# The block-diagonal stage of a long convolution, moved from full-array matmuls to sets of 32x32 array tiles

## The chip, the cores and the metric

The kernel runs on one core of one Trainium2 chip. The metric is device time in microseconds (us), measured for the whole execution; each kernel was run several times and the median is quoted. Every ratio below compares a kernel with the kernel before in the same rounds on the same chip. One core has no sibling cores to compare clocks with, so a run counts as undisturbed when it lies near the fastest of its kernel.

## The reference, cut to what matters

Two independent computations share the core. Part A is a gated long convolution over 2048 positions and 1024 channels, done by a transform of length 4096. Part B is a diagonal state space model (SSM) whose scan and dense products need none of A's results. The outputs are concatenated.

```python
# A: k_shift = short causal filter of k;  kv = k_shift * v
y_f = rfft(kv padded to 2S) * rfft(ssm_k padded to 2S)
y   = irfft(y_f)[:S] + kv * ssm_D
a   = q * y
# B: Bu = x @ B_bar^T ; h_t = Lam_bar * h_{t-1} + Bu_t ; y = 2 Re(h @ C^T) + x * Dskip
return concatenate([a, b], axis=-1)
```

## The kernel before

The transform is split into two steps. Step one multiplies by a dense 128-row matrix (stage A1) and writes a spectrum to DRAM (`Ys_kv`, `Ys_h`). Step two mixes only 32 numbers at a time (16 complex values), so 128 partitions hold four independent blocks, and its matrix is block-diagonal after a permutation. This middle stage, A2, loads both spectra, applies step two to each (`a2_s2`), multiplies them as complex numbers, applies the inverse of step two (`a2_sa`), and writes `Vs`. Stage A3 finishes the inverse. SSM work is interleaved with all of this by "ticks": the program puts operations on a list for each tick, and a scheduler then fixes each engine's order when it compiles.

The complex product needs real and imaginary halves exchanged. `ha` holds the filter's spectrum with the real parts in partitions 0 to 63 and the imaginary parts in 64 to 127; `hb` is the same with halves swapped, and the swap is two DMAs.

```python
    def dma(out_, in_):   return nc.sync.dma_start(out_, in_)     # issued by SP
    def dmas_(out_, in_): return nc.gpsimd.dma_start(out_, in_)   # issued by GpSimd (POOL)
    ...
    def a2_load(gq):                      # two of 32 groups at a time
        ...
        for nm, Ys in (("l2k", Ys_kv), ("l2h", Ys_h)):
            t_ = a2.tile([P, GC, D], BF16, name=nm, bufs=3)
            dma(t_[:], Ys.rearrange("c n (s g) d -> (c n s) g d", g=NG)[:, g0:g0 + GC, :])
        ...
        dma(wts[:], W3v[:, g0:g0 + GC, :, :])
    def a2_s2(g, src, dh):
        ...
        pt = ps_a.tile([P, 512], F32, name="psa")
        nc.tensor.matmul(pt[:], wts[:, gi, 0, :], s_[:, gi, dh * 512:(dh + 1) * 512], start=True, stop=True)
        nc.scalar.copy(d_[:, dh * 512:(dh + 1) * 512], pt[:])
        if src == 0 and dh == NH - 1:
            hb = a2.tile([P, D], BF16, name="hb", bufs=4)
            dmas_(hb[0:64, :], ha[64:128, :])
            dmas_(hb[64:128, :], ha[0:64, :])
    ...
    def a2_sa(g, dh):
        ...
        nc.tensor.matmul(pt[:], wts[:, gi, 1, :], ha[...], start=True, stop=False)
        nc.tensor.matmul(pt[:], wts[:, gi, 2, :], hb[...], start=False, stop=True)
        nc.scalar.copy(vsb[:, gi, dh * 512:(dh + 1) * 512], pt[:])
```

## Time and profile before

Median 431.73 us over three runs (428.91 to 433.8). I call "the stage" the time from the start of the first block-diagonal matmul to the start of the last one, read from the trace.

| before | value |
|---|---|
| stage | 190.4 to 361.8 us, 171.4 us, 16 pairs of groups |
| span of the profiled run | 431.1 us |
| busy in 183 to 366: TensorE / VectorE / ScalarE | 177.9 / 140.5 / 133.5 of 183 us |
| time after the stage | 69.3 us |

The view by windows gives, for each stretch, busy time and instruction count by engine, then the granted clock, the DMA share (1.0 would be all 16 DMA engines busy throughout) and the rate.

```profile
core 0: us, PE busy (x) PEld busy (x) DVE busy (x) ACT busy (x) POOL busy (x), PEclk, DMA share, GB/s
191.00:193.00 2.00, 2.00 (x23) 1.29 (x20) 2.00 (x5) 1.72 (x4) 0.57 (x2) 1.00 1.07 409
183.00:366.00 183.00, 177.91 (x1562) 110.92 (x1561) 140.51 (x241) 133.49 (x244) 47.49 (x89) 0.99 0.70 222
```

TensorE (PE) is busy for 178 of 183 us: it bounds the stage.

The timeline of TensorE (start, duration, source line, tiles, count) shows a full-array matmul here: the next instruction starts 0.216 us after it (241.70 to 241.92, 242.37 to 242.58).

```profile
241.70 0.38 PE L508 MATMUL psa<-l2h,wts 128*128 128x512 bf16 x1
241.92 0.61 PE L274 MATMUL pu<-xT,BT 128*128 128x128 bf16 x8
242.37 0.38 PE L532 MATMUL psa<-ha,wts 128*128 128x512 bf16 x1
242.58 0.38 PE L533 MATMUL psa<-hb,wts 128*128 128x512 bf16 x1
```

The page's list of DMA issues gives size and median time from issue to landing:

```profile
l2k<-Ys_kv SPq DMA_DIRECT2D x16, 512.0 KB, 6.0
l2h<-Ys_h SPq DMA_DIRECT2D x16, 512.0 KB, 4.2
hb<-ha POOLq DMA_DIRECT2D x64, 128.0 KB, 3.7
Vs<-vsb POOLq DMA_DIRECT2D x16, 512.0 KB, 5.9
```

### The profile page before, as it was taken

Reading aid. Unit: us, or ns where it says so; the run is one execution under the profiler, and the core shown is the slowest. Engines: PE = TensorE matmul, PEld = TensorE weight load, DVE = VectorE, ACT = ScalarE, POOL = GpSimd, SP = SyncE. Lnnn points to the kernel's source line nnn. Section 1 sums busy time; section 2 is a strip of 40 time slices with the busy share of each in tenths; the row PEclk is TensorE's granted clock in tenths of the full one; section 3 lists DMA queues with packets and bytes.
Section 4 is the critical chain, followed back from the end, with each engine's and each line's share of the span. In section 5 each row is a group of like instructions: output and inputs, shape, how many; then the busy total and the mean of one; then the engine's idle time right before and its main releaser. Section 6 shows DMA issues by size and latency. Waiting matters only on the chain.

```text
span 431.1 us, 9757 instructions
## 1 busy us (share of the span) xinstructions
PE 380.7 (88%) x3713; PEld 259.7 (60%) x3713; DVE 350.7 (81%) x642; ACT 303.6 (70%) x531; POOL 130.2 (30%) x224
## 2 busy tenths in 40 slices
PE   2589799797987997999899999999899999997784
PEld 2578687575765875775556566566465666763331
DVE  2989999999999999936897979797959637976830
ACT  1977999787886887646678877878568783344451
POOL 4000344464654455311222232322122211012121
PEclk9979999999999899999999999999899999999989
DMA  7879987778776544397778687879666523959981
GB/s 247 285 255 309 336 289 254 265 240 249 276 235 205 167 163 159 120 334 238 229 241 263 217 247 245 265 234 295 195 217 181 165 69 135 298 176 396 403 316 73
DMA packets 41353, 102.23 MB, mean 237 GB/s; under 512 B 6621, under 2 KB 8925, under 8 KB 41306
## 3 DMA queue, kind: packets, MB, share of 16 engines
q1 hardware_dynamic: 27322, 58.60, 42.7%
q0 software_dynamic: 13984, 43.01, 28.8%
q8 instruction: 29, 0.48, 0.5%
q14 instruction: 18, 0.15, 0.1%
HBM read 59.64 MB, written 33.55 MB: 216 GB/s over the span
## 4 chain that ended last, share of the span: by engine, by line
PE 42%; DVE 28%; issue 12%; DMA 10%; ACT 5%; POOL 2%; SPq 0%; POOLq 0%; DVEq 0%; ACTq 0%
PE pu L274 13%; PE py L345 13%; DVE m L409 5%; PE psa L508 5%; DVE acc L410 4%; DMA hb<-ha 3%; PE psa L533 3%; PE psa L532 3%; DVE ta L305 2%; DVE tb L308 2%; DVE acc L414 2%; DMA out_dram<-ot 2%; POOL out_dram L88 2%; DMA bn<-in_B_C_re_dram 1%; PE pt L601 1%
## 5 line engine op out<-in xcount | busy, mean ns | idle before, releaser
L274 PE MATMUL pu<-xT,BT 128*128 128x128 bf16 x2048 | 156.1, 222 | 0.5 <-ACT xT L263 0.3
L274 PEld LDWEIGHTS <-BT 128*128 128x128 bf16 x2048 | 136.2, 100 | 33.5 <-issue 2.4
L345 PE MATMUL py<-CT,h 128*128 128x512 bf16 x512 | 140.2, 382 | 2.3 <-ACT yo L355 2.3
L345 PEld LDWEIGHTS <-h 128*128 128x128 bf16 x512 | 46.7, 98 | 45.5 <-issue 4.9
L88 POOL DMA_DIRECT2D hb<-ha x64 | 33.4, 526 | 88.9 <-ACT ha L509 85.0
L534 ACT CAST vsb<-psa 128x512 bf16<-128x512 f32 x64 | 37.0, 602 | 25.7 <-PE psa L533 24.8
L88 POOL DMA_DIRECT2D Ys_h<-ysbh x64 | 45.6, 716 | 30.8 <-ACT ysbh L475 29.4
L277 ACT CAST u<-pu 128x512 bf16<-128x512 f32 x64 | 39.4, 615 | 13.2 <-PE pu L274 13.1
L428 ACT CAST ysb<-psa 128x512 bf16<-128x512 f32 x64 | 38.5, 644 | 13.7 <-PE psa L427 13.3
L519 DVE TENSOR_TENSOR ha<-x,ha 128x1024 bf16<-128x1024 bf16 x32 | 21.9, 684 | 27.8 <-DMA hb<-ha 18.7
L475 ACT CAST ysbh<-psa 128x512 bf16<-128x512 f32 x64 | 38.7, 641 | 5.5 <-issue 2.3
L509 ACT CAST ha<-psa 128x512 bf16<-128x512 f32 x64 | 36.8, 598 | 7.3 <-PE psa L508 6.3
L509 ACT CAST x<-psa 128x512 bf16<-128x512 f32 x64 | 36.9, 593 | 7.3 <-PE psa L508 5.2
L308 DVE TENSOR_TENSOR_SCAN tb<-rtab,tb 128x1024 bf16<-128x1024 f32 x16 | 36.6, 2285 | 0.0
L305 DVE TENSOR_TENSOR_SCAN ta<-rtab,ta 128x1024 bf16<-128x1024 f32 x16 | 36.5, 2280 | 0.0
L427 PE MATMUL psa<-acc,F1t 128*128 128x512 bf16 x64 | 24.6, 392 | 12.0 <-DVE acc L414 11.9
L564 ACT CAST ot<-psa 128x512 bf16<-128x512 f32 x32 | 17.9, 589 | 24.4 <-DMA out_dram<-ot 14.8
L409 DVE TENSOR_TENSOR m<-krow,wbc 128x1024 bf16<-128x1024 bf16 x48 | 32.4, 675 | 0.0
L410 DVE TENSOR_TENSOR acc<-acc,m 128x1024 bf16<-128x1024 bf16 x48 | 32.3, 673 | 0.0
L532 PE MATMUL psa<-ha,wts 128*128 128x512 bf16 x64 | 24.5, 384 | 4.2 <-DVE ha L519 4.0
L88 POOL DMA_DIRECT2D Ys_kv<-ysb x32 | 17.8, 557 | 33.9 <-ACT ysb L428 33.9
L350 PE MATMUL py<-Dd,xT 128*128 128x128 bf16 x128 | 28.0, 219 | 0.0
(139 smaller groups left out, 628.5 us busy)
## 6 DMA issues: line engine op xcount, KB each, us to landing
Ys_kv<-ysb POOLq DMA_DIRECT2D x32, 256.0 KB, 2.9
Ys_h<-ysbh POOLq DMA_DIRECT2D x64, 128.0 KB, 3.3
l2k<-Ys_kv SPq DMA_DIRECT2D x16, 512.0 KB, 6.0
l2h<-Ys_h SPq DMA_DIRECT2D x16, 512.0 KB, 4.2
hb<-ha POOLq DMA_DIRECT2D x64, 128.0 KB, 3.7
Vs<-vsb POOLq DMA_DIRECT2D x16, 512.0 KB, 5.9
vv<-Vs SPq DMA_DIRECT2D x32, 256.0 KB, 6.6
xn<-in_B_x_dram SPq DMA_DIRECT2D x16, 256.0 KB, 4.3
```

The costliest lines, as they stand in the source:

```text
L88: return nc.gpsimd.dma_start(out_, in_)
L274: nc.tensor.matmul(pu[:, c, jl, :], BT[:, j, c, dd, :], xT[:, dd, :], start=(dd == 0), stop=(dd == ND - 1))
L277: nc.scalar.copy(u[:, :, j - 1:j + 1, :], pu[:])
L305: ops.append(lambda: nc.vector.tensor_tensor_scan(fl(st["ta"]), fl(rtab), fl(st["ta"]), 0.0, ALU.mult, ALU.add))
L308: nc.vector.tensor_tensor_scan(fl(st["tb"]), fl(rtab), fl(st["tb"]), 0.0, ALU.mult, ALU.add)
L345: nc.tensor.matmul(py[:], h[:, c, j, :], CT[:, j, c, dh * 512:(dh + 1) * 512], start=(j == 0 and c == 0), stop=(j == NJ - 1 and c == 1))
L409: ops.append(lambda jj=jj: nc.vector.tensor_mul(st["m"][:], krows[n2 - jj][:], wbc[:, jj, :]))
L410: ops.append(lambda: nc.vector.tensor_add(st["acc"][:], st["acc"][:], st["m"][:]))
L428: nc.scalar.copy(ysb[:, dh * 512:(dh + 1) * 512], pt[:])
L475: nc.scalar.copy(ysbh[:, :, n2l, :], pt[:].rearrange("p (c d) -> p c d", c=2))
L509: nc.scalar.copy(d_[:, dh * 512:(dh + 1) * 512], pt[:])
L532: nc.tensor.matmul(pt[:], wts[:, gi, 1, :], ha[:, dh * 512:(dh + 1) * 512], start=True, stop=False)
```

## The change

The stage's weight matrix is three quarters zeros. The change drops the zeros: each 128x128 matmul becomes four matmuls of 32 partitions into 32 output rows, on four different 32x32 tiles of the array. Four groups together make a set of 16 tiles that covers the array and writes four PSUM banks. A unit is now four groups by 512 channels; there are again 16 units. To make it fit: block s must lie in partitions 32s to 32s+31, so the loads' source gets a separate dimension for s; the swap of halves becomes eight DMAs of 16 partitions; the transposes' PSUM pool gives one bank to the stage; and the DRAM spectra get a channel-half dimension.

```diff
-    ps_t = ctx.enter_context(tc.tile_pool(name="ps_t", bufs=2, space=PSUM))
+    ps_t = ctx.enter_context(tc.tile_pool(name="ps_t", bufs=1, space=PSUM))
-    ps_a = ctx.enter_context(tc.tile_pool(name="ps_a", bufs=3, space=PSUM))
+    ps_a = ctx.enter_context(tc.tile_pool(name="ps_a", bufs=4, space=PSUM))
 ...
-    Vs = tc.dram_tile([2, N2, P, D], BF16, name="Vs")          # Ys_kv, Ys_h alike
+    Vs = tc.dram_tile([NH, 2, N2, P, 512], BF16, name="Vs")
 ...
-            dma(t_[:], Ys.rearrange("c n (s g) d -> (c n s) g d", g=NG)[:, g0:g0 + GC, :])
+    ysv = {nm: t_.rearrange("h c n (s g) d -> h s (c n) g d", g=NG) ...}
+            dma(st[nm][:], ysv[nm][dh, :, :, qd * Q4:(qd + 1) * Q4, :])
 ...
+    def tiles16(outs, wt, rhs, u, inv, start, stop):
+        g0 = (u // NH) * Q4
+        for i in range(Q4):
+            for s_ in range(4):
+                a_, b_ = 32 * s_, 32 * ((s_ + i) % 4)
+                if inv:
+                    a_, b_ = b_, a_
+                nc.tensor.matmul(outs[i][b_:b_ + 32, :], a2state["w"][a_:a_ + 32, g0 + i, wt, :],
+                                 rhs[a_:a_ + 32, i, :], start=start, stop=stop)
 ...
-            dmas_(hb[0:64, :], ha[64:128, :])
-            dmas_(hb[64:128, :], ha[0:64, :])
+            for s_ in range(8):
+                o = s_ ^ 1
+                dmas_(hb[16 * s_:16 * s_ + 16, :, :], d_[16 * o:16 * o + 16, :, :])
 ...  (four evictions per set, products over 128x2048, one Vs store per unit, ticks per unit instead of per group)
```

More of the change, by code (lines that the diff above doesn't have):

```diff
@@ L34, in a_constants @@
     cph, sph = np.cos(phi), np.sin(phi)
-    W2 = np.zeros((2, 4, N2, NG, 2, 4, N2))
-    Wa = np.zeros((2, 4, N2, NG, 2, 4, N2))
-    Wb = np.zeros((2, 4, N2, NG, 2, 4, N2))
+    W3 = np.zeros((4, 2, N2, NG, 3, 2, N2))
     for si in range(4):
-        c_ = cph[si]; s_ = sph[si]
-        c_n2k2 = np.transpose(c_, (1, 0, 2)); s_n2k2 = np.transpose(s_, (1, 0, 2))
-        W2[0, si, :, :, 0, si, :] = c_n2k2
-        W2[1, si, :, :, 0, si, :] = s_n2k2
-        W2[0, si, :, :, 1, si, :] = -s_n2k2
-        W2[1, si, :, :, 1, si, :] = c_n2k2
-        c_k2n2 = np.transpose(c_, (2, 0, 1)); s_k2n2 = np.transpose(s_, (2, 0, 1))
-        Wa[0, si, :, :, 0, si, :] = c_k2n2
-        Wa[0, si, :, :, 1, si, :] = s_k2n2
-        Wa[1, si, :, :, 0, si, :] = -c_k2n2
-        Wa[1, si, :, :, 1, si, :] = -s_k2n2
-        Wb[0, si, :, :, 0, si, :] = -s_k2n2
-        Wb[0, si, :, :, 1, si, :] = c_k2n2
-        Wb[1, si, :, :, 0, si, :] = -s_k2n2
-        Wb[1, si, :, :, 1, si, :] = c_k2n2
+        for gi in range(NG):
+            c_, s_ = cph[si, gi], sph[si, gi]
+            r = (si + gi) % 4
+            W3[si, 0, :, gi, 0, 0, :] = c_
+            W3[si, 1, :, gi, 0, 0, :] = s_
+            W3[si, 0, :, gi, 0, 1, :] = -s_
+            W3[si, 1, :, gi, 0, 1, :] = c_
+            W3[r, 0, :, gi, 1, 0, :] = c_.T
+            W3[r, 0, :, gi, 1, 1, :] = s_.T
+            W3[r, 1, :, gi, 1, 0, :] = -c_.T
+            W3[r, 1, :, gi, 1, 1, :] = -s_.T
+            W3[r, 0, :, gi, 2, 0, :] = -s_.T
+            W3[r, 0, :, gi, 2, 1, :] = c_.T
+            W3[r, 1, :, gi, 2, 0, :] = -s_.T
+            W3[r, 1, :, gi, 2, 1, :] = c_.T
     f = lambda a: np.ascontiguousarray(a.reshape(128, -1), dtype=np.float32).astype(ml_dtypes.bfloat16)
-    W2 = np.transpose(W2, (0, 2, 1, 3, 4, 5, 6))
-    Wa = np.transpose(Wa, (0, 1, 2, 3, 4, 6, 5))
-    Wb = np.transpose(Wb, (0, 1, 2, 3, 4, 6, 5))
-    W3 = np.stack([W2.reshape(128, NG, 128), Wa.reshape(128, NG, 128), Wb.reshape(128, NG, 128)], axis=2)
     return f(F1), f(G), f(W3)
@@ L116, in full_kernel @@
     dma(Gt[:].rearrange("p c k -> p (c k)"), Gd.ap())
-    W3v = W3d.ap().rearrange("p (g t m) -> p g t m", g=NG, t=3)
-    Ys_kv = tc.dram_tile([2, N2, P, D], BF16, name="Ys_kv")
-    Ys_h = tc.dram_tile([2, N2, P, D], BF16, name="Ys_h")
-    Vs = tc.dram_tile([2, N2, P, D], BF16, name="Vs")
+    Ys_kv = tc.dram_tile([NH, 2, N2, P, 512], BF16, name="Ys_kv")
+    Ys_h = tc.dram_tile([NH, 2, N2, P, 512], BF16, name="Ys_h")
+    Vs = tc.dram_tile([NH, 2, N2, P, 512], BF16, name="Vs")
     praw = const.tile([4 * NJ, P], BF16, name="praw")
@@ L429, in a1_kv_mm @@
         if dh == NH - 1:
-            dmas_(Ys_kv[c, n2, :, :], ysb[:])
+            dmas_(Ys_kv[:, c, n2, :, :].rearrange("h k d -> k h d"), ysb[:].rearrange("k (h d) -> k h d", h=NH))
             A1.pop(("ysb", n2))
@@ L477, in a1h_mm @@
             for c in range(2):
-                dmas_(Ys_h[c, 2 * n2g:2 * n2g + 2, :, qd * DQ:(qd + 1) * DQ].rearrange("n k d -> k n d"), ysbh[:, c, :, :])
+                dmas_(Ys_h[qd // 2, c, 2 * n2g:2 * n2g + 2, :, (qd % 2) * DQ:(qd % 2 + 1) * DQ].rearrange("n k d -> k n d"), ysbh[:, c, :, :])
             A1.pop(("ysbh", qd, n2g))
@@ L481, in a1h_mm, with a2_load @@
                 A1.pop(("hT", qd, n2 // 4))
-    GC = 2
     a2state = {}
-    gstate = {}
-    def a2_load(gq):
+    Q4 = 4
+    ysv = {nm: t_.rearrange("h c n (s g) d -> h s (c n) g d", g=NG) for nm, t_ in (("l2k", Ys_kv), ("l2h", Ys_h))}
+    vsv = Vs.rearrange("h c n (s g) d -> h s (c n) g d", g=NG)
+    def a2_load(u):
         a2 = pools["a2"]
-        g0 = gq * GC
-        l2 = []
-        for nm, Ys in (("l2k", Ys_kv), ("l2h", Ys_h)):
-            t_ = a2.tile([P, GC, D], BF16, name=nm, bufs=3)
-            dma(t_[:], Ys.rearrange("c n (s g) d -> (c n s) g d", g=NG)[:, g0:g0 + GC, :])
-            l2.append(t_)
-        wts = a2.tile([P, GC, 3, P], BF16, name="wts", bufs=3)
-        dma(wts[:], W3v[:, g0:g0 + GC, :, :])
-        a2state[gq] = [l2[0], l2[1], wts, None]
@@ L499, in a2_s2 @@
-    def a2_s2(g, src, dh):
-        a2 = pools["a2"]
-        gq, gi = divmod(g, GC)
-        l2k, l2h, wts, _ = a2state[gq]
-        if src == 0 and dh == 0:
-            gstate[g] = [a2.tile([P, D], BF16, name="x16", bufs=4), a2.tile([P, D], BF16, name="ha", bufs=4), None]
-        x16, ha, _ = gstate[g]
-        s_, d_ = ((l2h, ha), (l2k, x16))[src]
-        pt = ps_a.tile([P, 512], F32, name="psa")
-        nc.tensor.matmul(pt[:], wts[:, gi, 0, :], s_[:, gi, dh * 512:(dh + 1) * 512], start=True, stop=True)
-        nc.scalar.copy(d_[:, dh * 512:(dh + 1) * 512], pt[:])
-        if src == 0 and dh == NH - 1:
-            hb = a2.tile([P, D], BF16, name="hb", bufs=4)
-            dmas_(hb[0:64, :], ha[64:128, :])
-            dmas_(hb[64:128, :], ha[0:64, :])
-            gstate[g][2] = hb
@@ L516, in a2_prod @@
-    def a2_prod(g, which):
-        x16, ha, hb = gstate[g]
-        if which == 0:
-            nc.vector.tensor_mul(ha[:], x16[:], ha[:])
-        else:
-            nc.vector.tensor_mul(hb[:], x16[:], hb[:])
-    def a2_sa(g, dh):
-        a2 = pools["a2"]
-        gq, gi = divmod(g, GC)
-        l2k, l2h, wts, vsb = a2state[gq]
-        if vsb is None:
-            vsb = a2.tile([P, GC, D], BF16, name="vsb", bufs=2)
-            a2state[gq][3] = vsb
-        x16, ha, hb = gstate[g]
-        pt = ps_a.tile([P, 512], F32, name="psa")
-        nc.tensor.matmul(pt[:], wts[:, gi, 1, :], ha[:, dh * 512:(dh + 1) * 512], start=True, stop=False)
-        nc.tensor.matmul(pt[:], wts[:, gi, 2, :], hb[:, dh * 512:(dh + 1) * 512], start=False, stop=True)
-        nc.scalar.copy(vsb[:, gi, dh * 512:(dh + 1) * 512], pt[:])
-        if dh == NH - 1:
-            gstate.pop(g)
-            if gi == GC - 1:
-                g0 = gq * GC
-                dmas_(Vs.rearrange("c n (s g) d -> (c n s) g d", g=NG)[:, g0:g0 + GC, :], vsb[:])
-                a2state.pop(gq)
+        qd, dh = divmod(u, NH)
@@ new lines, in a2_load @@
+        st = a2state[u] = {}
+        for nm in ("l2h", "l2k"):
+            st[nm] = a2.tile([P, Q4, 512], BF16, name=nm, bufs=3)
+            dma(st[nm][:], ysv[nm][dh, :, :, qd * Q4:(qd + 1) * Q4, :])
[6 more added lines that the diff above has]
+                    a_, b_ = b_, a_
+                nc.tensor.matmul(outs[i][b_:b_ + 32, :], a2state["w"][a_:a_ + 32, g0 + i, wt, :], rhs[a_:a_ + 32, i, :],
+                                 start=start, stop=stop)
@@ new lines, in a2_s2 @@
+    def a2_s2(u, src):
+        a2 = pools["a2"]
+        st = a2state[u]
+        nm = ("l2h", "l2k")[src]
+        d_ = st[("ha", "x16")[src]] = a2.tile([P, Q4, 512], BF16, name=("ha", "x16")[src], bufs=2)
+        pts = [ps_a.tile([P, 512], F32, name="psa") for _ in range(Q4)]
+        tiles16(pts, 0, st.pop(nm), u, False, True, True)
+        for i in range(Q4):
+            nc.scalar.copy(d_[:, i, :], pts[i][:])
+        if src == 0:
+            hb = st["hb"] = a2.tile([P, Q4, 512], BF16, name="hb", bufs=2)
+            for s_ in range(8):
+                o = s_ ^ 1
+                dmas_(hb[16 * s_:16 * s_ + 16, :, :], d_[16 * o:16 * o + 16, :, :])
@@ new lines, in a2_prod, with a2_sa @@
+    def a2_prod(u, which):
+        st = a2state[u]
+        t_ = st[("ha", "hb")[which]]
+        nc.vector.tensor_mul(t_[:], st["x16"][:], t_[:])
+    def a2_sa(u):
+        a2 = pools["a2"]
+        qd, dh = divmod(u, NH)
+        st = a2state.pop(u)
+        pts = [ps_a.tile([P, 512], F32, name="psa") for _ in range(Q4)]
+        tiles16(pts, 1, st["ha"], u, True, True, False)
+        tiles16(pts, 2, st["hb"], u, True, False, True)
+        vsb = a2.tile([P, Q4, 512], BF16, name="vsb", bufs=2)
+        for i in range(Q4):
+            nc.scalar.copy(vsb[:, i, :], pts[i][:])
+        dmas_(vsv[dh, :, :, qd * Q4:(qd + 1) * Q4, :], vsb[:])
@@ L548, in a3_load @@
             t_ = a3.tile([P, D], BF16, name=f"vv{c}", bufs=4)
-            dma(t_[:], Vs[c, n2, :, :])
+            dma(t_[:].rearrange("k (h d) -> k h d", h=NH), Vs[:, c, n2, :, :].rearrange("h k d -> k h d"))
             vv.append(t_)
@@ L722, in switch_a2 @@
             pools["a2"] = cms["a2"].__enter__()
+            a2state["w"] = pools["a2"].tile([P, NG, 3, 32], BF16, name="W3t", bufs=1)
+            dma(a2state["w"][:].rearrange("p g t m -> p (g t m)"), W3d.ap())
             a2_load(0)
@@ L726, in full_kernel @@
         a2_last = 0
-        for g in range(NG):
-            b = A2_T0 + g * A2_STEP
-            if g % GC == 0 and g // GC + 2 < NG // GC:
-                at(b, "misc", lambda g=g: a2_load(g // GC + 2))
-            for bi_, (src, dh) in enumerate([(0, 0), (0, 1), (1, 0), (1, 1)]):
-                at(b + bi_ // 2, "pe_a", lambda g=g, src=src, dh=dh: a2_s2(g, src, dh))
-            at(b + 3, "dve_a", lambda g=g: a2_prod(g, 0))
-            at(b + 3, "dve_a", lambda g=g: a2_prod(g, 1))
-            for dh in range(NH):
-                at(b + 5, "pe_a", lambda g=g, dh=dh: a2_sa(g, dh))
+        NU = NG // Q4 * NH
+        for u in range(NU):
+            b = A2_T0 + u * A2_STEP * 2
+            if u + 2 < NU:
+                at(b, "misc", lambda u=u: a2_load(u + 2))
+            at(b, "pe_a", lambda u=u: a2_s2(u, 0))
+            at(b + 1, "pe_a", lambda u=u: a2_s2(u, 1))
+            at(b + 3, "dve_a", lambda u=u: a2_prod(u, 0))
+            at(b + 3, "dve_a", lambda u=u: a2_prod(u, 1))
+            at(b + 5, "pe_a", lambda u=u: a2_sa(u))
             a2_last = max(a2_last, b + 5)
```

## The prediction

> **What bounds the kernel now.** The block-diagonal stage runs from about 183 us (first spectrum load) to 362 us (its last matmul), some 177 us for 16 pairs of groups, 11.1 us per pair. The busy time by window (183 to 366 us) gives TensorE 178 of 183 us, VectorE 141, ScalarE 133, granted clock 0.99. So TensorE bounds this stage; from 50 to 150 us VectorE does (49 of 50). In the timeline the stage's 128x512 matmuls start 0.216 us apart: 256 of them are 55 us of the 177; the rest is the SSM's.
>
> **What the change removes.** 256 full-array matmuls become 1024 of 32x32x512 in 64 sets of 16. [...] Weight loads fall from 3.1 MB to 0.8 MB.
>
> **What it does not remove.** ScalarE still makes 192 evictions of 128x512 (0.59 us each, the psum tile's view), VectorE the same products. Per unit of four groups, 12 evictions (7.1 us) now come in two ticks of four. Each set takes all four banks, so the next waits for evictions, 2.4 us per four. In the compiled order many sets are broken into fours of one bank between SSM matmuls; such fours should gain little. TensorE gives back most of its gain as waits on ScalarE. The halves' swap becomes 8 small DMAs per unit; at about 0.5 us of GpSimd issue each (0.524 now) the last is issued some 4 us after the first, and the products wait.
>
> **What I expect to decide: DMA engines.** The spectrum loads' source is no longer one stride over 128 rows: in the compiled program it is 4 x 32 x 2048 elements against 128 x 1 x 2048. [...] Saturated stretches show 391 to 404 GB/s at a share of 1.02 to 1.05, 24.5 GB/s an engine; a 4 KB packet takes 159 ns undisturbed. Per unit two 512 KB loads put 64 packets on each of four engines, 10.2 us; the swap, Vs stores and SSM traffic add about 3.2 us there. 13.4 us x 16 = 214 us, against 177: about +37 us, nearly all on the critical path since program order ties the SSM work to these ticks. Imperfect overlap, waits on the swap, one transpose bank instead of two at the start (+3 us) and 1 KB instead of 2 KB runs in Ys_kv stores and the last stage's loads (+2 us) add some 8 us.
>
> **Predicted: 476 us, 436 to 512 (8 in 10).** Faster by over 2%: 0.10; within 2%: 0.09; slower by over 2%: 0.81.
>
> **What would show it.** l2h and l2k landings rise from 4.2 and 6.0 us to 10 us or more; mean DMA share in the stage falls from 0.70 while tiled matmuls wait on these loads; the stage lasts 210 us or more; evictions keep 0.59 us; first transposes wait for evictions.
>
> **What would make it wrong.** If the loads still spread over 16 engines (landing under 7 us), bursts of evictions and the swap set the stage: 415 to 455 us. If moreover the sets of 16 overlap fully and waits are hidden, the next bounds are VectorE and ScalarE: about 410 to 420. If the Vs stores fall on four engines too and collide, over 500.

The sum: 431.7 before, 37 for the loads and 8 for the rest are the 476 us predicted. That the loads would get four engines no trace of the kernel before shows; the trace of the changed kernel does (a share of 0.27, below). The +3 and +2 us and the 8 us are estimates.

## More of the kernel before

While spectrum loads run (191 to 193), all 16 DMA engines are in use: a share of 1.07, at 409 GB/s.

The chain of work that ended last, by engine (shares of the span), is mostly TensorE and VectorE:

```profile
PE 42%; DVE 28%; issue 12%; DMA 10%; ACT 5%; POOL 2%; SPq 0%; POOLq 0%; DVEq 0%; ACTq 0%
```

## The result, and the profile after

The changed kernel takes 534.27 us (531.54 to 534.8). The ratio to the kernel before is 1.2346, with a 95% interval of 1.2251 to 1.2442. Such ratios are the mean time of one kernel's fast runs over that of the other's fast runs of the same rounds, so they are not quite the ratio of the quoted medians. Executions over 1.5% slower than the fastest of the same kernel are left out of the means. The direction was predicted; the size was not: 534 lies outside 436 to 512.

The windows show where the time is. The second line is the stage (199.3 to 459.1, 259.8 us instead of 171.4).

```profile
192.00:194.00 2.00, 2.00 (x28) 1.53 (x26) 0.00 (x0) 0.00 (x0) 0.00 (x0) 1.00 0.27 82
199.00:459.00 260.00, 217.65 (x2454) 115.78 (x2453) 163.93 (x247) 132.52 (x246) 77.86 (x153) 0.89 0.48 139
470.00:480.00 10.00, 4.69 (x25) 2.01 (x23) 0.00 (x0) 0.58 (x1) 0.56 (x1) 1.00 0.30 79
```

TensorE is now busy for 84% of the stage, not 97%. While little but spectrum loads runs (192 to 194), the DMA share is 0.27 at 82 GB/s: 0.27 x 16 = 4.3, about four of sixteen engines. Near the end of the inverse (470 to 480), while the last `Vs` stores land, the share is 0.30 at 79 GB/s: about four again (0.30 x 16 = 4.8).

The list of DMA issues. The page gives no landing time for the two loads (more on that below); the store's has doubled, and the swap's, at half the size, has doubled too:

```profile
l2h<-Ys_h SPq DMA_DIRECT2D x16, 512.0 KB
l2k<-Ys_kv SPq DMA_DIRECT2D x16, 512.0 KB
hb<-ha POOLq DMA_DIRECT2D x128, 64.0 KB, 7.2
Vs<-vsb POOLq DMA_DIRECT2D x16, 512.0 KB, 11.2
```

For the loads the trace has something better than the page: each increment of the semaphore that tells of a landing. A load of the kernel before makes 16 increments as it lands. Each of these loads makes one as its issue ends and four much later, which agrees with the four engines of the share. The last of the four comes 26.9 us (`l2h`) and 22.7 us (`l2k`) after the start of the issue, at the median, against 4.2 and 6.1 before.

The chain that ended last now runs through transfers, by engine and then by line:

```profile
DMA 34%; PE 23%; issue 13%; DVE 12%; ACT 12%; POOL 4%; SPq 1%; POOLq 0%; ACTq 0%; DVEq 0%
DMA l2h<-Ys_h 10%; DMA Vs<-vsb 10%; PE py L338 6%; PE pu L267 6%; PE psa L496 6%; DMA hb<-ha 5%; DMA Ys_h<-ysbh 4%; ACT ysbh L468 2%; DMA bn<-in_B_B_re_dram 2%; ACT vsb L528 2%; POOL out_dram L82 1%; ACT CT L618 1%; DVE ha L517 1%; DVE hb L517 1%; DVE ta L298 1%
```

The timeline of TensorE shows what became of the "sets of 16":

```profile
240.18 0.40 PE L496 MATMUL psa<-l2k,W3t 32*32 32x512 bf16 x4 [0.72 <-ACT vsb L528]
240.51 0.23 PE L267 MATMUL pu<-xT,BT 128*128 128x128 bf16 x1
240.67 0.40 PE L496 MATMUL psa<-l2k,W3t 32*32 32x512 bf16 x4
241.00 0.23 PE L267 MATMUL pu<-xT,BT 128*128 128x128 bf16 x1
...
242.19 0.39 PE L338 MATMUL py<-CT,h 128*128 128x512 bf16 x1
246.65 0.61 PE L496 MATMUL psa<-l2h,W3t 32*32 32x512 bf16 x4 [4.08 <-DMA l2h<-Ys_h]
```

The compiled order puts an SSM matmul between fours of one set, so each four pays its own time, 0.33 us here (240.18 to 240.51, 240.67 to 241.00). Then TensorE waits 4.08 us for a spectrum load.

Finally the waits of 189 to 471 us (engine, line and what ended the wait: total us, times, longest):

```profile
DVE h L316 <- PE py L338: 53.2, 9, 17.0
POOL hb L82 <- DMA Vs<-vsb: 50.3, 12, 7.9
PE psa L496 <- DMA l2h<-Ys_h: 10.5, 4, 4.1
```

GpSimd spends 50 us holding swap DMAs back until an earlier `Vs` store has landed. The trace shows what ties the two together. The program gives GpSimd's DMAs eight completion semaphores in turn (this order is never broken in the trace), and each of these 12 swap DMAs waits on the very semaphore that it is to raise itself, that is until the DMA eight places before it, the store, has landed. Eight swaps and a store are nine DMAs a unit, one more than there are semaphores; the kernel before has five, and none of its DMAs waits in this way. Direct waits of TensorE on a load add up to far less (10.5 us); the loss reaches it by detours.

An account by differences of the two profiled spans, 532.8 - 431.1 = 101.7 us: the stage starts 8.9 us later, is 88.4 us longer, and what follows is 4.4 us longer (73.7 against 69.3). Summing the steps from one matmul's start to the next inside the stage splits the 88.4: 39.3 are steps from one full-array SSM matmul (transposes included) to the next, and 338 more such steps now fall inside the stage (1340 against 1002); 49.1 are steps to, from and among block-diagonal matmuls. Steps over 1 us add up to 54.1 us against 3.9. So SSM work filled part of the slow stage, but running it early bought nothing: afterwards, from 463 to 532, TensorE is busy for only 40 of 69 us and yet that end is not shorter. The clock granted to TensorE fell too, from 0.99 to 0.89 in the stage. As a cause of its own it is not isolated, but two of the kernels below take the same time at different clocks: 507.53 us at a mean of 0.92 to 0.93, and 508.33 us at 0.96 to 0.97.

### The profile page after: what moved, and what is told of

Read it like the earlier page. It is cut to its first block, busy times and chain, and to the rows that moved or that the text cites. A ratio compares the mean times of both kernels' runs of the same rounds, so it can differ in the third digit from the quotient of the medians.

```text
span 532.8 us, 11271 instructions
## 1 busy us (share of the span) xinstructions
PE 417.4 (78%) x4481; PEld 255.4 (48%) x4481; DVE 353.1 (66%) x610; ACT 300.4 (56%) x531; POOL 165.7 (31%) x288
## 4 chain that ended last, share of the span: by engine, by line
DMA 34%; PE 23%; issue 13%; DVE 12%; ACT 12%; POOL 4%; SPq 1%; POOLq 0%; ACTq 0%; DVEq 0%
DMA l2h<-Ys_h 10%; DMA Vs<-vsb 10%; PE py L338 6%; PE pu L267 6%; PE psa L496 6%; DMA hb<-ha 5%; DMA Ys_h<-ysbh 4%; ACT ysbh L468 2%; DMA bn<-in_B_B_re_dram 2%; ACT vsb L528 2%; POOL out_dram L82 1%; ACT CT L618 1%; DVE ha L517 1%; DVE hb L517 1%; DVE ta L298 1%
## 5 line engine op out<-in xcount | busy, mean ns | idle before, releaser
L338 PE MATMUL py<-CT,h 128*128 128x512 bf16 x512 | 151.4, 402 | 9.0 <-ACT yo L348 9.0
L267 PEld LDWEIGHTS <-BT 128*128 128x128 bf16 x2048 | 131.8, 100 | 36.9 <-issue 18.6
L82 POOL DMA_DIRECT2D hb<-ha x128 | 61.5, 486 | 135.3 <-ACT ha L507 61.1
L496 PEld LDWEIGHTS <-W3t 32*32 32x32 bf16 x1024 | 18.1, 89 | 78.9 <-issue 60.4
L557 DVE TENSOR_TENSOR ot<-ot,qt 128x1024 bf16<-128x1024 bf16 x16 | 11.1, 692 | 58.9 <-ACT ot L553 58.9
L316 DVE TENSOR_TENSOR h<-ta,eor 128x1024 bf16<-128x1024 bf16 x16 | 11.0, 688 | 53.2 <-PE py L338 53.2
L468 ACT CAST ysbh<-psa 128x512 bf16<-128x512 f32 x64 | 37.2, 631 | 12.6 <-PE psa L467 6.2
L82 POOL DMA_DIRECT2D Ys_kv<-ysb x32 | 22.9, 716 | 53.4 <-ACT ysb L421 52.9
L496 PE MATMUL psa<-l2k,W3t 32*32 32x512 bf16 x256 | 26.5, 438 | 16.4 <-ACT vsb L528 13.2
L348 ACT CAST yo<-py 128x512 bf16<-128x512 f32 x32 | 19.5, 610 | 33.7 <-PE py L338 20.3
L285 DVE TENSOR_TENSOR ta<-u,ci 128x1024 bf16<-128x1024 bf16 x16 | 11.0, 685 | 40.3 <-ACT u L270 40.3
```

What stands on the lines that cost most here:

```text
L267: nc.tensor.matmul(pu[:, c, jl, :], BT[:, j, c, dd, :], xT[:, dd, :], start=(dd == 0), stop=(dd == ND - 1))
L338: nc.tensor.matmul(py[:], h[:, c, j, :], CT[:, j, c, dh * 512:(dh + 1) * 512], start=(j == 0 and c == 0), stop=(j == NJ - 1 and c == 1))
L348: nc.scalar.copy(yo[:, dh * 512:(dh + 1) * 512], py[:])
L468: nc.scalar.copy(ysbh[:, :, n2l, :], pt[:].rearrange("p (c d) -> p c d", c=2))
L496: nc.tensor.matmul(outs[i][b_:b_ + 32, :], a2state["w"][a_:a_ + 32, g0 + i, wt, :], rhs[a_:a_ + 32, i, :], start=start, stop=stop)
```

## The experiments

Eighteen kernels were run; all gave correct results. "Stage" is always first to last start of a block-diagonal matmul.

The theory at the outset (T1) was the prediction's: loads on four DMA engines. The rivals were the `Vs` stores on four engines (T2), the swap of eight DMAs behind GpSimd's queue (T3), large units that let the scheduler form long bursts of SSM matmuls (T4), and sets split between SSM matmuls (T5). The expectations below use other names: the "four-engine theory" is T1 with T2, the first "burst theory" is T3 to T5 in one, the "order theory" is T4, and the "fragment theory" is T5. Their "tile theory" has the tiles or the "mode switches", the steps between tiles and full-array matmuls, slow in themselves.

### First round: are the loads or the stores on four engines to blame?

**Loads in four DMAs of 32 partitions each**, so that each has one stride over its partitions:

```diff
-            dma(st[nm][:], ysv[nm][dh, :, :, qd * Q4:(qd + 1) * Q4, :])
+            for s_ in range(4):
+                dma(st[nm][32 * s_:32 * s_ + 32, :, :], ysv[nm][dh, s_, :, qd * Q4:(qd + 1) * Q4, :])
```

> Edit: each spectrum load becomes four loads of 32 partitions (source pattern 32 x 2048)[...]; same bytes, same 4 KB packets. Four-engine theory: DMA share while only these loads run goes from 0.27 to above 0.8, a load's parts land in under 6 us, and the kernel falls from 534 to 470-500 us, because the stores of Vs still land in 10 us and hold the swap's DMAs back. Burst theory (evictions in bursts, eight small swap DMAs, array mode switches set the unit's 17 us): within 2% of 534.

Measured: 523.9 us, ratio 1.216 (1.209 to 1.224), stage 257.8. The loads did spread, as this window shows, next to 0.27 and 82 GB/s in the same place of the changed kernel:

```profile
192.00:194.00 2.00, 2.00 (x28) 1.53 (x26) 0.00 (x0) 0.59 (x1) 0.00 (x0) 1.00 0.98 374
```

Yet only 10 us came back. Either the loads cost little, or another limit stood right behind them.

**`Vs` store in four DMAs of 32 partitions**, loads left as in the change:

```diff
-        dmas_(vsv[dh, :, :, qd * Q4:(qd + 1) * Q4, :], vsb[:])
+        for s_ in range(4):
+            dmas_(vsv[dh, s_, :, qd * Q4:(qd + 1) * Q4, :], vsb[32 * s_:32 * s_ + 32, :, :])
```

> Edit: each Vs store becomes four of 32 partitions; the loads stay as the change has them. Four-engine theory: stores land in 3-5 us instead of 11, the GpSimd waits for Vs landings (about 48 us in all in the stage) go, but two loads of 10.2 us a unit plus some 3 us of other packets on four engines stay as a floor of 13.4 us a unit: 480-510 us. Burst theory: 48 more GpSimd DMA issues of 0.5 to 0.7 us make it 534-550.

Measured: 559.75 us, ratio 1.298 (1.290 to 1.306), stage 294.5.

**Both edits.**

> Edit: loads and stores both split in four. Four-engine theory: nearly all of the loss goes: 435-460 us, stage 185-205 us; what is left over 432 is the bursts and the swap. Burst theory: 530 or more.

Measured: 551.7 us, ratio 1.282 (1.274 to 1.290), stage 287.5. These two misses taught something about the method. GpSimd's wait for a `Vs` store fell from 50.3 us to 15.5 and then out of the list of waits, as it should. But VectorE's wait for `py`, an SSM result, rose from 53.2 to 125.8 and 106.5 us. The number of DMAs is an input to the scheduler, and the compiled order of TensorE's instructions had changed too. An edit of DMAs alone was therefore not a clean experiment here. The order of matmuls in the traces differs from the change's in the run with four loads and in the run with the two-DMA swap below as well. I did not isolate which move of the order costs the 25 us, and so the cost of four-engine stores (T2) stays unmeasured by itself.

**Loads in two DMAs of 64 partitions**, source 2 x 32 rows, for which I expected two engines:

```diff
+            for s_ in (0, 2):
+                dma(st[nm][32 * s_:32 * s_ + 64, :, :], ysv[nm][dh, s_:s_ + 2, :, qd * Q4:(qd + 1) * Q4, :])
```

> Edit: each load becomes two of 64 partitions, source pattern 2 x 32 x 2048. Four-engine theory[...]: two engines[...], so 128 packets of 159 ns = 20.4 us a unit: share about 0.13 when only loads run, stage 330 us or more, kernel 590-680 us. If instead smaller or more numerous DMAs are what helps, it lies between the change (534) and the version with four loads. Burst theory: 534.

Measured: 668.86 us (two executions), ratio 1.553 (1.538 to 1.568), stage 392.7. In this run the traced order of TensorE's matmuls is exactly the change's, so here the loads alone differ. The window shows a share of 0.12, about two engines of sixteen (0.12 x 16 = 1.9):

```profile
192.00:194.00 2.00, 2.00 (x35) 1.88 (x33) 0.00 (x0) 0.59 (x1) 0.00 (x0) 1.00 0.12 39
```

The dose works: one load in four pieces, whole, and in two pieces (slowest source dimension 32, 4 and 2) gave shares of 0.98, 0.27 and 0.12, that is about 16, 4 and 2 engines. That these loads get few engines (T1) is shown, and with two it binds. With four something else held the kernel at almost the same time.

### Second round: the swap, the units' size

**Swap in two DMAs again.** Real and imaginary rows are interleaved by permuting the weights, so that the swap is even against odd partitions. The loads stay as in the change (share 0.27 there).

```diff
+    il = np.arange(2 * N2).reshape(2, N2).T.reshape(-1)
+    W3[:, :, :, 0, :] = W3[:, :, :, 0, :][..., il]      # and the inverse's input rows alike
 ...
-            for s_ in range(8):
-                o = s_ ^ 1
-                dmas_(hb[16 * s_:16 * s_ + 16, :, :], d_[16 * o:16 * o + 16, :, :])
+            dmas_(hb[0:P:2, :, :], d_[1:P:2, :, :])
+            dmas_(hb[1:P:2, :, :], d_[0:P:2, :, :])
```

> Edit on the change: real and imaginary rows interleaved inside each block of 32 (constants permuted), so the swap is two DMAs of 64 partitions (even to odd, odd to even) in place of eight of 16. Loads and stores stay on four engines. In the compiled order of TensorE, the SSM's matmuls that stand in unbroken stretches of more than 1.5 us [...] are 0.88 of all in the stage in the change, 0.05 before; here 0.77, and the longest falls from 8.6 to 6.6 us. Order theory (the block stage's 12 evictions a unit stand in a row in TensorE's program, about 8 us in which TensorE goes at ScalarE's pace, and the SSM's matmuls follow in one block, so the two add up): partly better, 480-510 us. Tile theory (32x32 tiles or mode switches themselves are slow): 530. Swap latency alone (fewer issues, less wait): 500-515.

Measured: 507.53 us, ratio 1.176 (1.169 to 1.182), stage 230.3. That is 27 us less than the change, with the loads still on four engines; not all of it need be the swap's, because TensorE's order changed with the edit. With the swap out of the way TensorE waits for `l2k` 14 times, 45.2 us in all: the loads come to the front.

**The same, and loads in four DMAs.**

> Edit: the two-DMA swap and loads in four of 32 partitions. Compiled order is now spread: 0.16 of the SSM's matmul time in long stretches. Order theory: 435-465 us, TensorE near 95% busy in the stage. Tile theory: 520 or more. Four-engine theory alone gave 2% for the loads, so it expects 2% under the run with the two-DMA swap alone.

Measured: 508.33 us, ratio 1.176 (1.171 to 1.182), stage 233.0: nothing gained over the run above, which none of the three expectations had. The waits on loads are gone, but the set is now chopped. Inside the stage TensorE returns 146 times from an unbroken stretch of tiles to full-array work, against 47 times in the run above and 104 in the change. The timeline of TensorE:

```profile
284.43 0.40 PE L501 MATMUL psa<-l2h,W3t 32*32 32x512 bf16 x4
284.76 1.07 PE L271 MATMUL pu<-xT,BT 128*128 128x128 bf16 x16
285.66 0.38 PE L342 MATMUL py<-CT,h 128*128 128x512 bf16 x1
285.97 0.39 PE L501 MATMUL psa<-l2h,W3t 32*32 32x512 bf16 x4
286.30 0.82 PE L342 MATMUL py<-CT,h 128*128 128x512 bf16 x3
```

From a tile to the next full-array instruction takes 0.33 us here (284.43 to 284.76), and the same after 285.97; the median over the stage is 0.317. From a 512-column full matmul to a tile takes 0.31 us (285.66 to 285.97), where another full-array instruction follows after 0.216. So an extra stretch costs 0.317 + 0.309 - 0.216 = 0.41 us. A lone four does the work of one full matmul, which costs 0.216.

**The same in units of two groups with four buffers** (finer units, against T4):

```diff
+    HB = 2
-        pts = [ps_a.tile([P, 512], F32, name="psa") for _ in range(Q4)]
+        pts = [ps_a.tile([P, 512], F32, name="psa") for _ in range(HB)]
 ...  (ha, hb, x16 of 128x2x512 with bufs=4; half a unit every two ticks)
```

> Edit: as the one before and in units of two groups (8 tiles in 2 banks at a time, working tiles half as big, four buffers in place of two, so the same bytes). Compiled order 0.13 in long stretches. Order theory: 420-445 us, the best of these, since sets wait for two evictions, not four. Tile theory: 520 or more.

Measured: 497.1 us, ratio 1.150 (1.141 to 1.159), stage 226.1. Finer units give 11 us, far from all: 497 lies between what the two theories expected.

**The kernel before with coarse units**: full-array matmuls, loads and swaps as before, but working tiles of two groups with two buffers, issued per pair.

```diff
-            gstate[g] = [a2.tile([P, D], BF16, name="x16", bufs=4), a2.tile([P, D], BF16, name="ha", bufs=4), None]
+            gstate[gq] = [a2.tile([P, GC, D], BF16, name="x16", bufs=2), a2.tile([P, GC, D], BF16, name="ha", bufs=2), None]
```

> Edit on the kernel before: the block stage's working tiles hold two groups of 1024 columns with two buffers in place of one group with four (same bytes), evictions and products in the change's order of events (two sets of four evictions, then four); full-array matmuls, 16-engine loads and stores, swap of two DMAs, three eviction banks, two transpose banks, all as before. Compiled order: 0.72 of the SSM's matmul time in long stretches (0.05 before). Order theory: 470-510 us without any tile or four-engine load. Tile theory and four-engine theory: 432 within 2%.

Measured: 437.3 us, ratio 1.011 (1.005 to 1.018), stage 169.9. Coarse units by themselves cost about 1%, where the order theory had expected 470 us or more. T4 fell here, together with a measure that had looked good. I had computed, from the compiled order, what share of the stage's SSM matmul time lies in unbroken stretches of over 1.5 us: 0.05 before, 0.88 in the change, 0.85 to 0.93 in the first round, in step with the times. But this run has 0.72 at 437 us, and the swap2-and-loads4 run above has 0.16 at 508 us. The correlation was an accident of the kernels tried first.

### Third round: fix TensorE's order

To test T5 the scheduler must not choose. The main loop was emitted with TensorE's order kept as written, each set whole, SSM matmuls between sets; the inverse moved from tick b+5 to b+6.

```diff
-            at(b, "pe_a", lambda u=u: a2_s2(u, 0))
+            for fn in (lambda u=u: a2_s2(u, 0), nop, nop):      # nops only space the interleaving
+                at(b, "pe_a", fn)
 ...
-    for t_ in range(-1, NT):
-        ...
+    with tc.manual_schedule(engines={nc.tensor.engine}):
+        for t_ in range(-1, NT):
+            ...
```

**On the kernel with two-DMA swap and four-DMA loads:**

> Edit on the run with two-DMA swap and loads in four: TensorE's program is kept in the order in which the kernel emits it, so every set of 16 tiles stands whole (one pair of mode switches a set, 47 stretches in place of 146) and three sets are spread evenly over four ticks; the last set of a unit one tick later. From the earlier traces a switch adds about 0.095 us to the step from one matmul to the next, and tiles of a set start 3 to 4 ns apart, so a whole set should cost 0.45-0.5 us against 0.86 for four full matmuls. Fragment theory (tiles are cheap when a set stays whole; split sets and mode switches ate the gain): stage 160-185 us, kernel 420-450. Tiles-slow theory: 490 or more.

Measured: 464.95 us, ratio 1.075 (1.070 to 1.080), stage 173.8. That is 43 us less than the same kernel in the scheduler's order, with the stage inside its expected range and the whole above it, and the returns fall from 146 to 47. The 99 stretches saved, at 0.41 us, are an estimated 41 us of the stage's 59; the edit fixes all of TensorE's order, so the rest may be other moves. The stage itself is now as short as before. The rest of the program is not: the stage starts at 211.4 instead of 199.4, because the kept order also binds stage A1 (the repaired version below, with the order kept in the stage alone, starts it at 190.6).

**The same order with full-array matmuls** of block-permuted 128x128 weights in place of the tiles. These weights are four times as large and are loaded per four groups, in eight more DMAs; that is part of what is compared.

```diff
-            for s_ in range(4): ...
-                nc.tensor.matmul(outs[i][b_:b_ + 32, :], a2state["w"][a_:a_ + 32, g0 + i, wt, :], ...)
+            nc.tensor.matmul(outs[i][:], a2state["w", u // NH][:, i, wt, :], rhs[:, i, :], start=start, stop=stop)
```

> The same kernel and TensorE order with each set as four full-array matmuls (block-permuted 128x128 weights, loaded per four groups). Fragment theory: TensorE has 64 x 0.4 = 25 us more to do than with whole tile sets, so 430-455 and 0 to 25 us slower than that run. Tiles-slow theory: 40 us or more faster than the tiled run.

Measured: 471.39 us, ratio 1.090 (1.086 to 1.094), stage 184.1. Whole sets are a gain over full matmuls, but of only 6.4 us; both runs are slower than expected.

**The change itself in the kept order** (eight-DMA swap, four-engine loads):

> The change as it is (eight-DMA swap, four-engine loads and stores) with TensorE's program in emission order as in the two runs above. Stacked-limits theory: whole sets take the mode switches away, but the loads' floor of 13.4 to 14.4 us a unit stays: stage 214-240 us, kernel 475-510. If the order alone were the cause: 440 or less.

Measured: 528.95 us, ratio 1.222 (1.216 to 1.227), stage 238.3. The expectation was 475 to 510 us: the stage lies in its range (214 to 240), but it starts at 212.1. Order alone mends 5 us. It is worth 43 us only where loads and swap are mended too.

**The kernel before with four-engine loads** (share 0.26 at 96 GB/s from 196 to 200 us). Only the order of the load's partitions and, to match, of the weights' rows is changed:

```diff
-    W2 = np.transpose(W2, (0, 2, 1, 3, 4, 5, 6))
+    W2 = np.transpose(W2, (1, 0, 2, 3, 4, 5, 6))
-            dma(t_[:], Ys.rearrange("c n (s g) d -> (c n s) g d", g=NG)[:, g0:g0 + GC, :])
+            dma(t_[:], Ys.rearrange("c n (s g) d -> s (c n) g d", g=NG)[:, :, g0:g0 + GC, :])
```

> The kernel before with its spectrum loads' source as 4 x 32 x 2048 (partition order and weight rows permuted, nothing else): the four-engine loads alone. By my prediction's sum, 10.2 us for two loads and some 3 us of other packets on those engines for each 11 us of stage: landing 10 us or more, stage 205-225 us, kernel 465-485. If four-engine loads don't bind: within 2% of 432.

Measured: 511.81 us, ratio 1.184 (1.180 to 1.189), stage 199.8 to 440.7, 240.9 us; expected was 465 to 485. This is the cleanest run: no tiles, no new swap, no DMA more or less, 159 stretches of block-diagonal matmuls as in the kernel before, and 79 us lost. The largest direct wait of TensorE is put down not to the spectrum loads but to the weights' load `wts`, which is issued among them. The waits of 183 to 441 us:

```profile
PE psa L508 <- DMA wts<-a_c_W: 68.9, 13, 14.0
```

The weights' load has one stride over 128 partitions and is unchanged. Its semaphore increments show why it is late. Twelve of its 16 shares land within 2.0 to 3.1 us of the end of the issue. The last four land 9 to 22 us after it, and the very last comes 0.3 to 1.2 us after the last share of the spectrum load that landed just before. The trace doesn't name engines, but this is what a load on all 16 looks like when four of them are still busy with earlier loads.

Are the four busy for the whole stage? The packets' times allow an estimate. In the 240.9 us of the stage the 4 KB packets of SP's queue, which are the spectrum loads, took 686 us in all, and all other packets 1212 us. If the others spread evenly over 16 engines, each of the four had 686 / 4 + 1212 / 16 = 247 us of packets: they were full throughout. Per unit that is 10.7 us for the loads and 4.7 for the rest.

The backlog also reaches SP. The timeline of its queue (start, duration of the issue):

```profile
189.76 7.13 SPq L85 DMA_DIRECT2D l2k<-Ys_kv  x1
196.94 5.44 SPq L85 DMA_DIRECT2D l2h<-Ys_h  x1
202.42 5.38 SPq L85 DMA_DIRECT2D wts<-a_c_W  x1
```

Of the 53 issues between 182 and 441 us, 16 took 2 to 10 us; in the stage of the kernel before none took over 0.55 us. But these long issues are not what makes `wts` late: in six units its issue took 0.32 us, and its last share still landed 11 to 21 us afterwards. Why SP stands in an issue is not in the trace.

### Fourth round: swap at fixed order, the PSUM bank, a repaired version

**Four-DMA loads, eight-DMA swap, kept order** (the kernel of 464.95 us with the change's swap put back):

```diff
-            dmas_(hb[0:P:2, :, :], d_[1:P:2, :, :])
-            dmas_(hb[1:P:2, :, :], d_[0:P:2, :, :])
+            for s_ in range(8):
+                o = s_ ^ 1
+                dmas_(hb[16 * s_:16 * s_ + 16, :, :], d_[16 * o:16 * o + 16, :, :])
```

> Edit on the change: loads in four of 32 partitions and TensorE's emission order, whole sets; the eight-DMA swap and four-engine stores stay. It differs from the 465 us run in the swap alone. If the eight-DMA swap costs by its own latency: 15-45 us slower than 465 (480-510). If it cost only through the compiled order: 462-475.

Measured: 504.46 us, ratio 1.164 (1.158 to 1.170), stage 218.2. At fixed order (the traced order of matmuls is the same in both runs), and with loads in four DMAs (share 0.98 in the first round), the eight-DMA swap costs 39.5 us. The waits show how: swap DMAs wait for the `Vs` store to land.

```profile
POOL hb L82 <- DMA Vs<-vsb: 68.6, 10, 9.2
```

With the two-DMA swap this line is absent from the waits. Again each of the ten waits is for the DMA eight places before, on the same semaphore; all waits of that kind in the stage, for stores, swaps and outputs, are 25 with 80.2 us, against none in the 464.95 us kernel. So it is the number of GpSimd's DMAs per unit, over eight semaphores, together with a slow store, that costs. Seven DMAs for the swap, or a faster store with the eight, were not tried.

**The kernel before with the change's PSUM split** (one bank for transposes, four for the stage):

```diff
-    ps_t = ctx.enter_context(tc.tile_pool(name="ps_t", bufs=2, space=PSUM))
+    ps_t = ctx.enter_context(tc.tile_pool(name="ps_t", bufs=1, space=PSUM))
-    ps_a = ctx.enter_context(tc.tile_pool(name="ps_a", bufs=3, space=PSUM))
+    ps_a = ctx.enter_context(tc.tile_pool(name="ps_a", bufs=4, space=PSUM))
```

> Edit on the kernel before: one transpose bank instead of two, four eviction banks instead of three, nothing else. Predicted in the blind text as +3 us. The tiled runs start the stage 4 to 10 us later than before (first set at 195-200 us against 190). If the bank does it: first matmul of the stage 3 to 9 us later and kernel 433-442; if the 1 KB stores do it: 432.

Measured: 436.76 us, ratio 1.011 (1.006 to 1.017); the stage starts at 194.4 instead of 190.4. The bank costs 4 us before the stage.

**Everything repaired**: tiles, two-DMA swap, loads and stores in four DMAs, order kept only within the stage, and PSUM banks split 2 and 3 outside it, 1 and 4 inside.

```diff
+        def switch_a2(): ...
+            ps_open(1, 4)      # and ps_open(2, 3) after the stage
 ...
+    for t_ in range(-1, A2_T0 - 3):
+        tick(t_)
     with tc.manual_schedule(engines={nc.tensor.engine}):
-        for t_ in range(-1, NT):
+        for t_ in range(A2_T0 - 3, a2_last + 1):
+            tick(t_)
+    for t_ in range(a2_last + 1, NT):
+        tick(t_)
```

> All repairs together: tiles, two-DMA swap, loads and stores in four, TensorE's order kept in the block stage alone (not before and after it, where keeping it delayed the stage's start to 211 us), two transpose banks and three eviction banks outside the stage. Stage 155-175 us, start at 190-195, tail 70-76: kernel 415-442. If all the limits named so far are the whole loss, it is within 2% of before or faster.

Measured: 431.81 us (431.61 without the slow execution) against 432.54 before, ratio 0.996 (0.992 to 1.001): the same. The stage is 162.5 us, 9 less than before, and the part after it 73.8 us, 4.5 more. `Vs` stores land in 3.7 us. In the timeline of TensorE the sets are whole, and two sets in a row start only 0.22 us apart, the time of one full matmul:

```profile
275.13 0.43 PE L509 MATMUL psa<-ha,W3t 32*32 32x512 bf16 x16
275.35 0.42 PE L509 MATMUL psa<-hb,W3t 32*32 32x512 bf16 x16
275.94 1.67 PE L350 MATMUL py<-CT,h 128*128 128x512 bf16 x7 [0.16 <-issue]
```

**The same with full-array matmuls** (the edit of the 471.39 us kernel):

> As the run before, with four full-array matmuls a set: what the tiles themselves are worth when nothing else differs. TensorE has 64 x 0.4 = 25 us more in the stage; where other waits hide part of it, 5 to 25 us slower than the tiled one.

Measured: 444.37 us, ratio 1.025 (1.021 to 1.030), stage 177.8. So in the repaired program the tiles, with their smaller weights, are worth 12.6 us, and the structure that they need costs about as much against the kernel before.

### Fifth round: can the shorter stage be used?

If TensorE has time to spare in the stage, units could come more often: **every three ticks**, and **seven ticks for two units**, instead of one every four. Both runs also put the inverse at tick b+5 again, where the repaired kernel has b+6.

```diff
-            b = A2_T0 + u * A2_STEP * 2
+            b = A2_T0 + u * 3             # the other run: (u * 7) // 2
```

> As the repaired tiled kernel, with a unit every three ticks in place of four, so that the block stage takes less of the SSM's work along and leaves more of it for the last stage, where TensorE is 22 of 37 us busy. TensorE's work in the stage falls to some 78 us of SSM matmuls and 30 us of sets; ScalarE's 12 evictions a unit (7.1 us) and its SSM copies then set about 8.5 us a unit: stage 135-155 us, kernel 412-432. If the swap's latency or the Vs stores bind: stage stays near 160 us and the kernel 432-445.

> As before with seven ticks for two units: between the two, 415-432 us; same if the stage does not shrink.

Measured: 444.73 us (ratio 1.034, 1.028 to 1.040) and 443.05 us (1.028, 1.023 to 1.033). The first has a stage of 150.9 us, the shortest of all, but what follows takes 99.8 us instead of 73.8, with TensorE busy for 83 of the last 99. The second has a stage of 162.4 and 87.9 after it. The SSM work that no longer fits into the stage comes later. What bounds that last part was not tested further. Neither run reached the 412 to 432 us hoped for, and no version beats the kernel before clearly.

## Why the prediction was wrong, point by point

It predicted 476 us with 436 to 512 as its range, and "slower by over 2%" at 0.81. Slower was right; 534 is 22 us beyond the upper end. Two terms of the sum failed: "about +37 us" for the loads on four engines, which measured alone are 79 us, and "some 8 us" for the swap and the rest, where the swap alone is 39.5 us at fixed order. A third, the sets broken into fours, was not in the sum.

**What bounds the kernel before: right.** TensorE is busy for 178 of the 183 us, and nothing in the runs contradicts it.

**"What I expect to decide: DMA engines": right count, wrong size.** The prediction assumed four engines for these loads, and the runs agree: shares of 0.27 for a slowest source dimension of 4, 0.12 for 2, 0.98 for 32, and four late increments of the semaphore for 4. Only these three forms and the kernel before (128, a share of 1.07) were compared, so no general rule is shown. The mis-sized term is "about +37 us". Measured alone, on the kernel before, four-engine loads cost 79 us. By the profiled spans these 79 are 69.5 in the stage, 9.4 before its start, and nothing after it. The 69.5 exceed 37 for two reasons. The sum took 177 us as the stage's length from the first load on, where matmul to matmul it is 171.4. And it took 13.4 us per unit as a floor that would be reached. The three kernels with four-engine loads and no worse limit had 14.4 to 15.1 us per unit (230.3, 238.3 and 240.9 us over 16). The trace of the clean run says which part was short: 10.7 us for the loads against 10.2 in the sum, and 4.7 us of other packets on the same engines (both estimates, from the packets' times) against 3.2. That the four engines would be full is borne out by this estimate; the other traffic on them was undercounted, and the 16-engine loads behind them came late as well.

**"Some 8 us" for the swap and the rest: too small.** At fixed order the eight-DMA swap alone costs 39.5 us. The prediction counted GpSimd's issue time, 4 us per unit. It did not count completion semaphores: with nine DMAs a unit over eight of them, a swap waits for the `Vs` store, itself on about four engines (a share of 0.30) and landing in 11 to 12 us. Its last sentence did name a branch: "If the Vs stores fall on four engines too and collide, over 500". The first half came true and should have had more weight, since the store's destination has the same 4 x 32 x 2048 shape as the loads' source. Whether stores and loads collided on the same engines is not shown.

**"TensorE gives back most of its gain": it gave back more than the gain.** The prediction had read the compiled order, saw that sets are broken into fours, and wrote that "such fours should gain little". A four costs 0.41 us where the full matmul costs 0.216: that term was counted as zero and is negative. With swap and loads mended, the order with whole sets is worth 43 us (508.33 to 464.95); the stretches saved are an estimated 41 us of the 59 by which the stage shrinks. The waits on ScalarE that the prediction named instead are there, but small: 13.2 us in the stage. Within a set tiles are cheap: they start 3 to 4 ns apart in the trace. But each change between tiles and full-array matmuls has a price there: tile to full-array is 0.317 against 0.216 us, and full-array to tile 0.309 against 0.216, so about 0.1 us each way. With 104 returns from tiles in the change, they were a cost to look for.

**Smaller terms: nearly right.** Evictions nearly kept their time: the page's means are 0.60 to 0.65 us for the stage's three kinds against 0.59 to 0.60. One transpose bank cost 4 us against 3 predicted. The last part grew by 4.4 us against 2.

**Why the sum could not have worked.** The terms are not additive. The nearest thing to a table of all combinations (medians in us; loads on "4 engines" are those of the change, share 0.27, on "16" those split into four DMAs, share 0.98; stores as in the change):

| loads | swap | scheduler's order | kept order |
|---|---|---|---|
| 4 engines | 8 DMAs | 534.3 (the change) | 529.0 |
| 16 engines | 8 DMAs | 523.9 | 504.5 |
| 4 engines | 2 DMAs | 507.5 | not run |
| 16 engines | 2 DMAs | 508.3 | 465.0 |

In the scheduler's column the order itself differs from row to row, so its differences are not of one edit alone. Mending one limit alone gives 5 to 27 us. Mending all three gives 69. Mending stores, PSUM split and the order outside the stage gives the last 33, to 431.8. Each of three limits was by itself enough for a stage of 218 us or more: loads 240.9, swap (with its four-engine store) 218.2, order 233.0. So removing the first mostly showed the second.

**What stays open.** Why more stores were slower by 25 to 28 us in the scheduler's order was not isolated: only that the compiled order changed with them. How much SP's long issues add to the 79 us, beyond the full engines, was not separated. The cost of the four-engine stores by themselves, at a fixed order, was not measured. What bounds the end of the two denser versions is not known.

## What to carry to other kernels

When a layout for packed matmuls adds a dimension in front of a DMA's partitions, check how many DMA engines that DMA gets, for loads and stores alike, and what else has to pass through the same engines; here the loads fell to a share of 0.27, and this alone cost 79 us, where the tiles were worth 12.6. When an edit turns one DMA into many, count them against the completion semaphores that the program takes in turn (nine over eight here, 39.5 us, with a slow store among them). Here packed tiles paid only in whole sets: keep their order, because an extra return to full-array matmuls and back costs 0.41 us, where a set can save at most 0.64 (four full matmuls of 0.216 against 0.22). And where a fix brings back little, suspect a second limit at the same height before discarding the cause, and fix the instruction order before comparing edits of DMAs.
